# A one-core kernel of attention and two MoE layers: softmax reciprocals one group later, warm-up matmuls, a shared PSUM bank and one TensorE visit per attention group

## The chip, the cores and the metric

The kernel runs on one core of one Trainium2 chip. The metric is device time of one execution in microseconds (us), the median of a few runs. A core has TensorE (PE, the matmuls), VectorE (DVE), ScalarE (ACT), GpSimd (POOL) and SyncE (SP), which run side by side and meet at semaphores; DMA queues move data between DRAM and the on-chip SBUF. Matmul results stand in PSUM, 8 banks of 128 partitions by 2 KB.

## What is computed

Three stages follow each other, cut here to what matters:

```python
def _attn_ref(q_l, k_l, v_l, q_g, k_g, v_g):        # batch 4, 8 heads, 512 local + 32 global, D 64
    out_g = np.matmul(sm(scale * q_g @ k_all.T), v_all)
    s_ll = np.where(np.abs(pos[:, None] - pos[None, :]) <= 32, s_ll, -1e9)
    out_l = np.matmul(sm(np.concatenate([s_lg, s_ll], axis=-1)), np.concatenate([v_g, v_l], axis=2))
    return np.concatenate([out_g, out_l], axis=2)
def _moe_ref(x, w1, w2, w3, w_out):                  # 2304 tokens, 512 -> 768 -> 512
    return np.maximum(np.maximum(x @ w1, x @ w2), x @ w3) @ w_out
def _moe2_ref(x, w_in, w_out):                       # 512 -> 2048 -> 512
    h = x @ w_in
    return (np.maximum(h, 0.0) + np.log1p(np.exp(-np.abs(h)))) @ w_out
```

`sm` is a softmax that divides by the sum plus 1e-9. The weights are float64 in DRAM (two 32-bit words each).

## The kernel before

**Attention.** The work is cut into 32 groups (4 batches, 2 halves of the sequence, 4 pairs of heads), numbered k = 0 to 31. A group goes through steps that stand in different turns of one generator, `att_stream`: `s1` (PE scores ps, DVE adds the mask and takes the minimum, L155, four per group), `s1e` (ACT exponentials, L162), `s1f` (DVE reciprocals rs of the sums, L168 and L169, and POOL's two multiplications by them, L171 and L172), `s2` (PE transposes pw, L218, and pg, L219), `s2e` (ACT and DVE copy these to pgt and pwt), `s3` (PE output po, L245 and L249), `s3h` (ACT: high part xh of the output, or xo to DRAM) and `s3l` (DVE: low part xl, L270). Every second group also serves the global queries: `s1g` (PE psg), `gsoft` (its softmax, tile gsc), `g2` (PE transposes pb, L279, and pa, L283) and `g3` (PE output pog, L297).

**First MoE.** A product of float32 precision is made of three matmuls of high and low parts (L504 to L506 and L550 to L552). There are 8 units u of 256 or 288 token columns. `up` makes one of 18 products pu of a unit (6 slices f, 3 weights i), 12 matmuls each; `rest` takes the maximum over i (ACT copies the first, DVE L518 the others); `split_h` makes hh and hl of the maximum; `down` makes two output slices pd with 36 matmuls each, which ACT copies to o (L555).

**Decoder.** `dec_stream` turns 24 float64 weight tiles into two float32 parts. For each tile ACT takes a magnitude (L448), DVE makes four steps (L462, L465, L469, L473; the middle two in the PSUM tile pt), and ACT and POOL write the two parts of w (L442, L443).

**Order.** All engines' streams are issued in the order of the Python code. First, until the inputs of units 0 and 1 are there (groups 0 to 10, the *opening* below), the driver walks `att_stream` and, between its steps, hands out decode steps (`part`) and some `up`s of unit 0 (`slot`). Groups 0 to KS-1 run in a fused form with two stops per group; the others in an order written out as letters in `ORD`, each letter a step of its own. Then comes the *run*: the remaining `up`s of units 0 and 1 (36 in all) with 2.3 decode steps behind each. Then units 0 to 7 go through `up` and `down`, and `more` lets attention steps in between by a rate (RA per `up`, RD per `down`), until attention ends. The second MoE decodes its weights the same way.

**PSUM.** Pool pm has 5 banks for everything that comes from `ptile` and for pu, pd, pt, pw, pg, pa, pb and psg; pool pp holds ps (two banks) and one bank with the tag "o" for po and pog in turn.

Of the kernel before, what the change touches and what calls it, by code (L numbers as in the profile page):

```python
# [7 lines left out]
F32 = mybir.dt.float32  # L8
# [12 lines left out]
def body(ctx, tc, kq, vw, vb, qg, w1, w2, w3, w_out, w2_in, w2_out, out):  # L21
# [4 lines left out]
    WM = 0  # L26
    KL = 10
    KW = 9
    KS = 8
    ORD = 'AHaBbFDIEG'  # L30
    HHA = 2
    HLP = 2
# [5 lines left out]
    pm = mo_ctx.enter_context(tc.tile_pool(name="pm", bufs=5, space=PSUM))  # L38
# [7 lines left out]

    ident = const.tile([128, 128], F32, name="ident")
# [163 lines left out]
    def s2(k):  # L211
# [4 lines left out]
        pg = ptile([128, 128], "pg")  # L216
# [20 lines left out]
    def s3(k):  # L237
# [3 lines left out]
        po = pp.tile([128, 4, 64], F32, tag="o", name="po", bufs=1)  # L241
# [30 lines left out]
    def g2(b, s):  # L272
# [4 lines left out]
        pb = ptile([128, 128], "pb")  # L277
# [10 lines left out]
    def g3(b, s):  # L288
# [3 lines left out]
        po = pp.tile([128, 2, 32], F32, tag="o", name="pog", bufs=1)  # L292
# [14 lines left out]
    def att_stream():  # L307
# [16 lines left out]
        for k in range(n + 3):  # L324
# [3 lines left out]
            if k < KS:  # L328
# [11 lines left out]
                if q3 is not None:  # L340
                    s3h(q3)
                yield 2 if k > 1 else 4
                next(soft, None)
# [3 lines left out]
                if q2 is not None:  # L347
                    s2e(q2)
                s1f(k)
# [12 lines left out]
                yield 3  # L362
            else:
                for c in ORD:
                    if c in "AaBb":
                        if k < n:
                            (s1 if c in "AB" else s1e)(k, "AaBb".index(c) // 2)
                            if c in "ab":
                                yield 0
                        if c in "AB":  # L370
                            next(soft, None)
                    elif c == "H":
                        if late:
                            g3(*late.pop())
                            ng += 1
                            yield 0
                    elif c == "D":
                        while p3 < p2 and p3 <= k - 2:
                            s3(p3)
                            s3h(p3)  # L380
                            s3l(p3)
                            p3 += 1
                            yield 0
                    elif c == "F":
                        if k < n:
                            s1f(k)
                            yield 0
                        next(soft, None)
                    elif c == "G":
                        if k < n and k % 2 == 1:  # L390
                            s1g(k)
                            yield 0
                    elif c == "E":
                        while p2 <= min(k - 1, n - 1):
                            s2(p2)
                            s2e(p2)
                            p2 += 1
                            yield 0
                    elif c == "I" and 2 <= k < n + 2:
                        b, hf, pr = groups[k - 2]  # L400
                        if hf == 1 and pr % 2 == 1:
                            g2(b, pr // 2)
                            yield 0
                            late.append((b, pr // 2))
# [29 lines left out]
    def dec_stream(srcs, wpool, rpool, pre, raws, staged):  # L434
# [22 lines left out]
        for i in range(n):  # L457
# [6 lines left out]
            t2 = ptile([128, 512], "pt").bitcast(I32) if staged else t  # L464
# [61 lines left out]
    def split_h(u, f):  # L526
# [9 lines left out]
        (nc.gpsimd if HLP > u else nc.vector).tensor_tensor(hl[:, f, 0:n], m, hh[:, f, 0:n].bitcast(F32), op=ALU.subtract)  # L536
# [72 lines left out]
    with tc.manual_schedule():  # L609
# [7 lines left out]
        AD = 5  # L617
        D0 = 0.5
        D2 = 2.0
        D3 = 1.0  # L620
        NS = 1
        MG = 1
        F2 = 5
        F6 = 1.2
        F7 = 2.0
        CX = 0
        FD = 3
        RJ = 0.7
        RD = 2.0
        RA = 1.9  # L630
        au = [0]
        nx = [0.0]
        debt = [0.0]

        def step():
# [439 lines left out]
```

## Time and profile before

| | us |
|---|---|
| median of 3 runs (811.77 to 813.16) | 812.82 |
| the profiled execution | 813.12 |
| its span in the trace | 811.4 |
| PE busy in it | 778.8 |
| DVE, ACT, POOL busy | 524.2, 423.7, 173.6 |

The profiled execution is 0.3 us above the median, and its trace spans 811.4 us of it. The stages by the clock of the trace: the opening until 66.5, the run of `up`s of units 0 and 1 until 119.8, `down` of unit 0 and the split of unit 1 until 155.5, the rest of attention beside units 1 to 4 until 318.3, then the end of the first MoE and the second one. A busy time of PE counts a matmul as long as its modelled end; what it lacks to a stretch's length is idle time of PE.

### The profile page before, as it was taken

What the parts mean: (1) busy time and instruction counts of PE and PEld (TensorE: products, weight loads), DVE (VectorE), ACT (ScalarE), POOL (GpSimd) and SP (SyncE); (2) the same over time, 40 slices, a digit from 0 to 9 for tenths busy, and PEclk for the clock granted to TensorE, in tenths of its full rate; (3) what the DMA queues carried; (4) which work ended last, traced back from release to release, by engine and by line L of the source; (5) the groups of instructions that cost most, each with busy time, mean ns of one, the idle gap of its engine ahead of it and who ended that gap; (6) DMA issues with size and microseconds to landing.
All of it is one profiled execution on the core that took longest, in us unless ns stands there. A gap on an engine that the chain in (4) does not pass through costs nothing.

```text
span 811.4 us, 17312 instructions
## 1 busy us (share of the span) xinstructions
PE 778.8 (96%) x6600; PEld 730.4 (90%) x6600; DVE 524.2 (65%) x1350; ACT 423.7 (52%) x1032; POOL 173.6 (21%) x183
## 2 busy tenths in 40 slices
PE   5689988999999999999998999999999999999998
PEld 3578987988989998999998889988999999999998
DVE  5867962455454453377746455655437989999996
ACT  5744534433433441324322688888878744444443
POOL 4434533211211120022223033433312200000000
PEclk9999999999999999999999999999999999999999
DMA  9827314433433411526020445544625734444421
GB/s 339 311 87 256 148 53 123 141 123 101 147 108 112 153 48 48 205 107 214 15 65 15 165 151 170 179 158 155 210 88 179 247 95 130 130 131 130 130 80 65
DMA packets 72403, 111.89 MB, mean 138 GB/s; under 512 B 9984, under 2 KB 51840, under 8 KB 72320
## 3 DMA queue, kind: packets, MB, share of 16 engines
q1 hardware_dynamic: 72320, 110.78, 40.8%
q8 instruction: 52, 0.85, 0.4%
q14 instruction: 31, 0.25, 0.1%
HBM read 80.67 MB, written 30.08 MB: 136 GB/s over the span
## 4 chain that ended last, share of the span: by engine, by line
PE 86%; DVE 6%; ACT 3%; DMA 2%; issue 1%; POOL 0%; SPq 0%; DVEq 0%; ACTq 0%; POOLq 0%
PE pu L504 8%; PE ph L976 8%; PE ph L978 8%; PE ph L977 8%; PE pu L505 7%; PE pu L506 7%; PE mb L863 7%; PE mb L864 7%; PE mb L862 7%; PE pd L550 3%; PE pd L551 3%; PE pd L552 3%; PE ps L149 2%; ACT s L162 2%; PE po L245 2%; DMA raw<-in_w_dram 2%
## 5 line engine op out<-in xcount | busy, mean ns | idle before, releaser
L504 PE MATMUL pu<-xh,w 128*128 128x288 f32 (+1 forms) x576 | 172.3, 299 | 5.3 <-DVE tmp L473 4.8
L505 PE MATMUL pu<-xl,w 128*128 128x288 f32 (+1 forms) x576 | 167.4, 291 | 0.0
L506 PE MATMUL pu<-xh,w 128*128 128x288 f32 (+1 forms) x576 | 166.7, 289 | 0.0
L863 PE MATMUL mb<-wo,oh 128*128 128x256 f32 x480 | 135.8, 283 | 0.0
L864 PE MATMUL mb<-wo,ol 128*128 128x256 f32 x480 | 135.7, 283 | 0.0
L862 PE MATMUL mb<-wo,oh 128*128 128x256 f32 x480 | 135.2, 282 | 0.0
L504 PEld LDWEIGHTS pu<-xh,w 128*128 128x128 f32 x576 | 109.6, 190 | 11.0 <-issue 5.4
L976 PE MATMUL ph<-o,w 128*128 128x384 f32 (+1 forms) x320 | 115.2, 360 | 0.5 <-ACT o L555 0.5
L978 PE MATMUL ph<-o,w 128*128 128x384 f32 (+1 forms) x320 | 115.0, 360 | 0.0
L977 PE MATMUL ph<-o,w 128*128 128x384 f32 (+1 forms) x320 | 115.0, 359 | 0.0
L505 PEld LDWEIGHTS pu<-xl,w 128*128 128x128 f32 x576 | 109.8, 191 | 0.0
L506 PEld LDWEIGHTS pu<-xh,w 128*128 128x128 f32 x576 | 109.6, 190 | 0.0
L984 DVE SCALAR_TENSOR_TENSOR g<-ph,a 128x384 f32<-128x384 f32 (+1 forms) x80 | 48.8, 610 | 88.5 <-ACT a L983 64.0
L855 ACT ACTIVATE oh<-sm 128x640 fp32r<-128x640 f32 (+1 forms) x72 | 49.8, 692 | 89.6 <-DVE sm L850 83.8
L862 PEld LDWEIGHTS mb<-wo,oh 128*128 128x128 f32 x480 | 91.7, 191 | 0.0
L864 PEld LDWEIGHTS mb<-wo,ol 128*128 128x128 f32 x480 | 91.3, 190 | 0.0
L863 PEld LDWEIGHTS mb<-wo,oh 128*128 128x128 f32 x480 | 91.2, 190 | 0.0
L162 ACT ACTIVATE s<-s,nm 128x160 f32<-128x160 f32 x128 | 53.4, 419 | 56.4 <-DVE nm L155 56.3
L443 POOL TENSOR_TENSOR w<-tmp,w 128x512 fp32r<-128x512 f32 x40 | 53.1, 1328 | 128.9 <-ACT w L442 82.5
L518 DVE TENSOR_TENSOR m<-m,pu 128x256 f32<-128x256 f32 (+1 forms) x96 | 41.7, 434 | 56.4 <-PE pu L506 50.6
L171 POOL TENSOR_TENSOR s<-s,rs 128x512 f32<-128x512 f32 x32 | 33.4, 1044 | 165.1 <-DVE rs L169 87.8
L976 PEld LDWEIGHTS ph<-o,w 128*128 128x128 f32 x320 | 60.2, 188 | 6.5 <-ACT o L555 0.7
(125 smaller groups left out, 1584.7 us busy)
## 6 DMA issues: line engine op xcount, KB each, us to landing
gl<-gd SPq DMA_DIRECT2D x32, 512.0 KB, 5.1
kq<-in_kq_dram SPq DMA_DIRECT2D x31, 448.0 KB, 4.4
raw<-in_w_out_dram SPq DMA_DIRECT2D x22, 512.0 KB, 4.1
raw<-in_w_dram SPq DMA_DIRECT2D x18, 512.0 KB, 7.6
gd<-g SPq DMA_DIRECT2D x48, 192.0 KB, 2.5
vt<-in_vw_dram SPq DMA_DIRECT2D x16, 512.0 KB, 5.5
raw<-in_w_in_dram SPq DMA_DIRECT2D x16, 512.0 KB, 7.5
gd<-g SPq DMA_DIRECT2D x32, 256.0 KB, 3.9
```

The lines of the kernel that those rows point to most:

```text
L162: nc.scalar.activation(s[:, u, :], s[:, u, :], AF.Exp, scale=-1.0, bias=g["nm"][:, u:u + 1], accum_out=g["sm"][:, u:u + 1])
L443: nc.gpsimd.tensor_tensor(w[:, 1, :], tf, w[:, 0, :].bitcast(F32), op=ALU.subtract)
L504: nc.tensor.matmul(p, lhsT=w[:, 0, k], rhs=xh[:, k, 0:n], start=(k == 0), stop=False)
L505: nc.tensor.matmul(p, lhsT=w[:, 0, k], rhs=xl[:, k, 0:n], start=False, stop=False)
L506: nc.tensor.matmul(p, lhsT=w[:, 1, k], rhs=xh[:, k, 0:n], start=False, stop=(k == 3))
L855: nc.scalar.activation(oh[:, a:b], src, AF.Copy)
L862: nc.tensor.matmul(p, lhsT=oh[:, a], rhs=w[:, 0], start=st, stop=False, skip_group_check=True)
L863: nc.tensor.matmul(p, lhsT=oh[:, a], rhs=w[:, 1], start=False, stop=False, skip_group_check=True)
L864: nc.tensor.matmul(p, lhsT=ol[:, a], rhs=w[:, 0], start=False, stop=sp, skip_group_check=True)
L976: nc.tensor.matmul(p, lhsT=w[:, 0, k], rhs=oh[:, 0:n], start=(k == 0), stop=False)
L977: nc.tensor.matmul(p, lhsT=w[:, 0, k], rhs=ol[:, 0:n], start=False, stop=False)
L978: nc.tensor.matmul(p, lhsT=w[:, 1, k], rhs=oh[:, 0:n], start=False, stop=(k == 3))
```

## The change

1. **Fused form for groups 0 to 10** (KS from 8 to 11), and in it `s1f` of group k-1 stands behind the exponentials of group k (it stood behind those of its own group); `s2e` of the group before moves ahead of the stop at which decode steps are handed out.
2. **One visit per later group.** `ORD` is gone. From group 11 on, `s1`, `s3`, `s2` and `s1g` are issued in one step; the exponentials, `s1f`, `g3` and `g2` are the following steps. RD and RA, the rates at which steps are let in, go from 2.0 and 1.9 to 1.4 and 1.35, AD from 5 to 3.
3. **Warm-up matmuls.** 18 matmuls on `ones` at the start (WM), 12 behind the scores of group 0 and 6 behind those of group 1 (WB); no one reads their results.
4. **PSUM.** Pool pm has 4 banks, a new pool pt has one for the decoder's middle steps, and one bank `acc` is shared by po (columns 0 to 255), pg (256 to 383), pb (384 to 511) and pog (0 to 63).
5. **Decode steps of the opening.** No decode step in group 0, one in group 1, three per group to group 8, five in groups 9 and 10, with two `up`s behind each of these (NSL). Both kernels hand out 32 in the opening.
6. **hl of unit 0 and 1.** On POOL only for unit 0, f below 3; the nine others move to DVE (before, all twelve were on POOL).

```diff
-    KS = 8
-    ORD = 'AHaBbFDIEG'
+    KS = 11
...
-    pm = mo_ctx.enter_context(tc.tile_pool(name="pm", bufs=5, space=PSUM))
+    pm = mo_ctx.enter_context(tc.tile_pool(name="pm", bufs=4, space=PSUM))
+    pt = mo_ctx.enter_context(tc.tile_pool(name="pt", bufs=1, space=PSUM))
...
+    acc = pp.tile([128, 512], F32, tag="o", name="acc", bufs=1)
...
-        pg = ptile([128, 128], "pg")
+        pg = acc[:, 256:384]
...
-        po = pp.tile([128, 4, 64], F32, tag="o", name="po", bufs=1)
+        po = acc[:, 0:256].rearrange("p (u n) -> p u n", n=64)
...
-        pb = ptile([128, 128], "pb")
+        pb = acc[:, 384:512]
...
-        po = pp.tile([128, 2, 32], F32, tag="o", name="pog", bufs=1)
+        po = acc[:, 0:64].rearrange("p (a n) -> p a n", n=32)
...
+                if k:
+                    s1f(k - 1)
+                next(soft, None)
+                if q2 is not None:
+                    s2e(q2)
                 yield 2 if k > 1 else 4
-                next(soft, None)
                 if q3 is not None:
                     s3l(q3)
                     p3 += 1
-                if q2 is not None:
-                    s2e(q2)
-                s1f(k)
...
-                for c in ORD:
...
+                if k == KS:
+                    s1f(k - 1)
+                if k < n:
+                    s1(k, 0)
+                    s1(k, 1)
+                while p3 < p2 and p3 <= k - 2:
+                    s3(p3)
+                    s3h(p3)
+                    s3l(p3)
+                    p3 += 1
+                while p2 <= min(k - (2 if k == KS else 1), n - 1):
+                    s2(p2)
+                    s2e(p2)
+                    p2 += 1
+                if k < n and k % 2 == 1:
+                    s1g(k)
+                next(soft, None)
+                yield 0
+                for i in range(2):
+                    if k < n:
+                        s1e(k, i)
+                        yield 0
+                    next(soft, None)
+                if k < n:
+                    s1f(k)
+                    yield 0
...
-            t2 = ptile([128, 512], "pt").bitcast(I32) if staged else t
+            t2 = pt.tile([128, 512], F32, tag="t", name="t2").bitcast(I32) if staged else t
...
-        (nc.gpsimd if HLP > u else nc.vector).tensor_tensor(hl[:, f, 0:n], m, hh[:, f, 0:n].bitcast(F32), op=ALU.subtract)
+        (nc.gpsimd if u == 0 and f < HLP else nc.vector).tensor_tensor(hl[:, f, 0:n], m, hh[:, f, 0:n].bitcast(F32), op=ALU.subtract)
...
-                part(D2)
+                part(D2 if cnt < 8 else D2L)
...
-                part(D3 if cnt > 1 else 3.0)
-                for _ in range(NS):
+                part(D3 if cnt < 8 else D3L)
+                for _ in range(NS if cnt < 8 else NSL):
...
-                if cnt > 8 and au[0] and ready(0):
-                    flush()
-                    slot(0)
-            cnt += 1
+                cnt += 1
+            elif cnt == 0:
+                warm(WB)
```

The first place is DVE's stream from the start of the program. Before, the scores of groups 0 and 1 (L155), each followed by its reciprocals, then the decode steps of the first tile:

```order
L155 ISA nm 128x1
L168 TENSOR_SCALAR rs<-sm 128x4
L169 RECIPROCAL rs<-rs 128x4
L462 TENSOR_SCALAR tmp<-tmp 128x512
L155 ISA s,nm<-ps,mask 128x160
...
L168 TENSOR_SCALAR rs<-sm 128x4
L169 RECIPROCAL rs<-rs 128x4
L465 TENSOR_SCALAR pt<-tmp 128x512
L469 SCALAR_TENSOR_TENSOR pt<-raw,pt 128x512
L473 SCALAR_TENSOR_TENSOR tmp<-raw,pt 128x512
```

After, the scores of groups 0 and 1 stand together (the lines move by a few numbers; t_294 is the decoder's tile in its own bank):

```order
L156 ISA s,nm<-ps,mask 128x160
L156 ISA nm 128x1
...
L169 TENSOR_SCALAR rs<-sm 128x4
L170 RECIPROCAL rs<-rs 128x4
L156 ISA s,nm<-ps,mask 128x160
...
L169 TENSOR_SCALAR rs<-sm 128x4
L170 RECIPROCAL rs<-rs 128x4
L460 TENSOR_SCALAR tmp<-tmp 128x512
L463 TENSOR_SCALAR t_294<-tmp 128x512
```

The reciprocals now stand behind a whole group of scores, and the first decode step behind three groups.

The second place is PE between `up`s and `down`s of the first units. Before, a group's work comes in separate pieces between products pu:

```order
L245 MATMUL po<-pgt,vb 64x128 x4
L249 MATMUL po<-pwt,vt 64x64 x8
L504 MATMUL pu<-xh,w 128x256
...
L218 MATMUL pw<-ident,s 128x128 x4
L219 MATMUL pg<-ident,sg 128x128
L184 MATMUL psg<-kq,qg 64x256 x2
L504 MATMUL pu<-xh,w 128x256
...
L149 MATMUL ps<-kq 64x160 x8
```

After, the same pieces of a group stand in a row:

```order
L150 MATMUL ps<-kq 64x160 x8
L246 MATMUL acc<-pgt,vb 64x128 x4
L250 MATMUL acc<-pwt,vt 64x64 x8
L219 MATMUL pw<-ident,s 128x128 x4
L220 MATMUL acc<-ident,sg 128x128
L185 MATMUL psg<-kq,qg 64x256 x2
L502 MATMUL pu<-xh,w 128x256
```

Interruptions of the products by attention fall in number, and the transposes pw of a group now stand right behind the outputs po of the group before.

The third place is ACT behind `down` of unit 0. Before, the split of unit 1 (hh) came ahead of the copies of the attention's output:

```order
L162 ACTIVATE s,sm<-s,nm 128x160 x4
L533 ACTIVATE hh<-m 128x288 x6
L262 ACTIVATE xo<-po 128x256
L230 ACTIVATE pgt<-pg 128x128
L193 ACTIVATE gsc<-psg 128x288
L555 ACTIVATE o<-pd 128x288 x2
```

After:

```order
L553 ACTIVATE o<-pd 128x256 x2
L163 ACTIVATE s,sm<-s,nm 128x160 x2
L263 ACTIVATE xo<-acc 128x256 x2
L231 ACTIVATE pgt<-acc 128x128
L194 ACTIVATE gsc<-psg 128x288
L531 ACTIVATE hh<-m 128x288 x6
```

There the copies xo, pgt and gsc stand ahead of hh, which unit 1's `down` waits for.

## Rows read from the trace of the kernel before

**Rows 1.** Busy time by stretch: us, engines (count), PEclk, DMA share, GB/s

```profile
5.20:21.90 16.70, 11.04 (x124) 7.62 (x126) 11.88 (x52) 11.47 (x43) 5.90 (x8) 1.00 1.01 393
21.90:43.70 21.80, 15.07 (x209) 11.76 (x203) 17.45 (x66) 14.62 (x53) 11.88 (x14) 0.92 0.79 281
43.70:66.50 22.80, 20.52 (x297) 18.01 (x296) 15.45 (x56) 12.99 (x45) 6.25 (x7) 1.00 0.24 80
66.50:119.80 53.30, 48.50 (x363) 47.49 (x361) 45.31 (x86) 24.58 (x50) 27.43 (x24) 0.97 0.44 165
119.80:155.50 35.70, 32.90 (x353) 28.91 (x352) 12.22 (x54) 16.82 (x62) 10.32 (x14) 0.95 0.36 112
155.50:318.30 162.80, 161.43 (x1877) 145.99 (x1873) 79.96 (x299) 64.43 (x231) 24.82 (x34) 1.00 0.34 109
```

**Rows 2.** DVE in the run: start, us, line, operation [idle before <-releaser]

```profile
80.72 0.42 DVE L462 TENSOR_SCALAR tmp<-tmp 128x512 f32<-128x512 f32 x1
83.24 0.42 DVE L462 TENSOR_SCALAR tmp<-tmp 128x512 f32<-128x512 f32 x1
...
110.41 0.43 DVE L462 TENSOR_SCALAR tmp<-tmp 128x512 f32<-128x512 f32 x1 [1.80 <-ACT tmp L448]
```

**Rows 3.** PE at the end of the run

```profile
113.31 0.40 PE L504 MATMUL pu<-xh,w 128*128 128x288 f32 x1 [2.18 <-DVE tmp L473]
```

**Rows 4.** DVE in the opening: the scores of group 4, and one reciprocal's first half

```profile
21.96 0.31 DVE L155 CUSTOM_DVE_ANT_0 s<-ps,mask 128x160 f32<-128x160 f32 x1
...
29.08 0.92 DVE L168 TENSOR_SCALAR rs<-sm 128x4 f32<-128x4 f32 x1
```

**Rows 5.** DVE, groups of 21.9 to 66.5: shapes, count | busy us, mean ns | idle before

```profile
L168 DVE TENSOR_SCALAR rs<-sm 128x4 f32<-128x4 f32 x7 | 1.9, 276 | 1.6 <-ACT s L162 1.6
```

**Rows 6.** PE in the opening

```profile
38.55 0.66 PE L283 MATMUL pa<-ident,gsc 128*128 128x128 f32 x4 [1.80 <-DVE tmp L473]
...
40.10 0.41 PE L505 MATMUL pu<-xl,w 128*128 128x256 f32 x1
...
57.30 0.66 PE L245 MATMUL po<-pgt,vb 128*64 128x128 f32 x8 [1.77 <-DVE xl L270]
```

**Rows 7.** PE around one `down` of unit 2's stretch

```profile
200.13 0.39 PE L504 MATMUL pu<-xh,w 128*128 128x256 f32 x1
...
201.76 0.66 PE L245 MATMUL po<-pgt,vb 128*64 128x128 f32 x8
...
202.81 0.39 PE L550 MATMUL pd<-hh,w 128*128 128x256 f32 x1
203.03 0.28 PE L551 MATMUL pd<-hl,w 128*128 128x256 f32 x1
...
207.08 0.28 PE L552 MATMUL pd<-hh,w 128*128 128x256 f32 x1
```

**Rows 8.** POOL, groups of 0 to 160

```profile
L443 POOL TENSOR_TENSOR w<-tmp,w 128x512 fp32r<-128x512 f32 x24 | 30.9, 1289 | 35.3 <-ACT w L442 30.7 <-issue 4.6
L171 POOL TENSOR_TENSOR s<-s,rs 128x512 f32<-128x512 f32 x16 | 16.7, 1041 | 46.0 <-DVE rs L169 23.1 <-DVE gsm L206 9.7 <-ACT w L442 5.9
```

**Rows 9.** DVE, groups of 119.8 to 318.3

```profile
L518 DVE TENSOR_TENSOR m<-m,pu 128x256 f32<-128x256 f32 x21 | 8.8, 419 | 19.3 <-PE pu L506 16.3 <-ACT gsc L204 2.4 <-DMA kq<-in_kq_dram 0.6
...
L536 DVE TENSOR_TENSOR hl<-m,hh 128x256 fp32r<-128x256 f32 x10 | 4.3, 433 | 0.3
```

**Rows 10.** All engines at the split of unit 1

```profile
137.39 2.09 ACT L533 ACTIVATE hh<-m 128x288 fp32r<-128x288 f32 x6
...
137.87 0.40 PE L550 MATMUL pd<-hh,w 128*128 128x288 f32 x1 [0.62 <-ACT hh L533]
...
139.39 0.36 ACT L262 ACTIVATE xo<-po 128x256 f32<-128x256 f32 x1
139.43 4.57 POOL L536 TENSOR_TENSOR hl<-m,hh 128x288 fp32r<-128x288 f32 x6
...
140.27 0.40 PE L551 MATMUL pd<-hl,w 128*128 128x288 f32 x1 [2.00 <-POOL hl L536]
```

More of the change, by code (lines that the diff above doesn't have):

```diff
@@ L24, in body @@
     scale = 1.0 / float(D) ** 0.5
-    WM = 0
+    WM = 18
     KL = 10
     KW = 9
-    KS = 8
-    ORD = 'AHaBbFDIEG'
+    KS = 11
     HHA = 2
-    HLP = 2
+    HLP = 3
     XLP = 0
@@ L361, in att_stream @@
                         late.append((b, pr // 2))
-                yield 3
+                yield 3 if k else 4
             else:
-                for c in ORD:
[L365 to L404, printed above, removed]
@@ new lines, in att_stream @@
+                next(soft, None)
[8 more added lines that the diff above has]
+                    yield 0
+                for c in late:
+                    g3(*c)
+                    ng += 1
+                    yield 0
+                late = []
+                if k < n + 2:
+                    b, hf, pr = groups[k - 2]
+                    if hf == 1 and pr % 2 == 1:
+                        g2(b, pr // 2)
+                        late.append((b, pr // 2))
+                        yield 0
@@ L616, in body @@
         FJ = 2.3
-        AD = 5
-        D0 = 0.5
+        AD = 3
         D2 = 2.0
@@ L621, in body @@
         NS = 1
+        D2L = 3.0
+        D3L = 2.0
+        NSL = 2
+        WB = 6
         MG = 1
@@ L628, in body @@
         RJ = 0.7
-        RD = 2.0
-        RA = 1.9
+        RD = 1.4
+        RA = 1.35
         au = [0]
@@ L673, in body @@
                 au[0] += 1
-                continue
-            if v == 2:
+            elif v == 2:
                 flush()
-                part(D2)
-            elif v == 4:
-                continue
+                part(D2 if cnt < 8 else D2L)
             elif v == 3:
-                part(D3 if cnt > 1 else 3.0)
-                for _ in range(NS):
+                part(D3 if cnt < 8 else D3L)
+                for _ in range(NS if cnt < 8 else NSL):
                     if au[0] and ready(0):
                         slot(0)
-            else:
-                part(D0)
-                if cnt > 8 and au[0] and ready(0):
-                    flush()
-                    slot(0)
-            cnt += 1
+                cnt += 1
+            elif cnt == 0:
+                warm(WB)
         flush()
```

## The prediction

> **What bounds the kernel now.** I read the busy times by stretch first, then the idle time of PE inside the stretches, then the rows of the engine that ends each pause. PE is busy 778.8 of 811.4 us, so what can be won at once is the idle time, the slowed matmuls, and whatever a switch between kinds of matmul costs. The stretches [rows 1] say where. In 5.2 to 21.9 PE has work for 11.0 of 16.7 us, the DMA share is 1.01 and DVE is busy 11.9: the inputs of the first groups pace it. In 21.9 to 66.5 PE idles 9.0 us and DVE is busy 32.9 of 44.6, so idle 11.7. In the run, 66.5 to 119.8, DVE is busy 45.3 of 53.3, and most of its other time is two pauses near the end: one decoded tile takes 83.24 - 80.72 = 2.52 [rows 2], and 16 of them fill 40.3. DVE's decoding paces the run; a late tile costs PE 2.18 there [rows 3], because DVE itself had waited 1.80 for the magnitude of a tile whose raw words came late [rows 2]. Behind the run PE idles 2.8 in the split of unit 1, and from 155.5 to 318.3 only 1.4 in all [rows 1]. From 318.3 on the change leaves the order as it was, and I take those 493.1 us as they are; the pool of four PSUM banks is short only where more than four products stand open, which the lag of two does not make.
>
> The granted clock falls three times. It is 0.92 in 21.9 to 43.7, 0.97 in the run and 0.95 in 119.8 to 155.5 [rows 1]; a matmul of this kind that takes 0.28 at full clock [rows 7] takes 0.41 there [rows 6], so PE stood at the lower of its two levels (1.2 instead of 2.4 GHz). Each time a pause of 1.8 to 2.2 us lay a few us ahead [rows 3, 6, 10]. The price of one such fall is (1 - 0.92) x 21.8 = 1.7 us.
>
> The sum is made against the profiled execution, 813.1; the median of the runs is 0.3 lower.
>
> **Part 1, the opening and the run.** *What happens until group 4.* By the scores of group 4, which start at 21.96 [rows 4], DVE has done ten decode steps in the kernel before; in the new order it has five. That is 5 x 0.63 (a quarter of 2.52) = 3.15 less in front of it, and one reciprocal pair (0.35) less. The gain lies between 0 (the inputs set the pace: DMA share 1.01 [rows 1]) and 3.5. I take 1.3, nearer the lower end for that DMA row: group 4 at 20.7.
>
> The warm-up matmuls lie in time in which PE waits for these inputs, and I cost them at nothing; their cover is 5.7 us of idle PE in that stretch. If they bought full clock for the first groups' scores, these still wait for inputs: nothing either way, and at worst group 4 comes 0.8 later, which lies inside the bounds.
>
> *From group 4 to the run.* DVE was busy 32.9 there. The new order has 23 decode steps until the last input of unit 1 where there were 21 (+1.3), one copy pwt (-0.7) and one maximum (-0.4) less, and the reciprocal that took 0.92 instead of 0.17 [rows 4] is taken as normal (-0.7): 32.4. Of its idle 11.7, the 1.6 before reciprocals [rows 5] goes, since rs now stands a group behind its exponentials; the rest I leave in size. New waits arise in the shared bank: pog of groups 8 and 10 and pb of 9 have to wait until DVE has read the low part xl out of the bank, and xl stands behind the decode steps handed out at that stop. The nearest row is po waiting 1.77 for xl [rows 6], in the one bank that po and pog shared already. Waits of DVE of the same kind are in the 11.7, so I keep 10.1. The run's DVE part starts at 20.7 + 32.4 + 10.1 = 63.2.
>
> *The run.* Then 17 tiles remain (seven are done) at 2.52: 42.8. The maxima and the three hl that move to DVE there are 23; what one adds is at most (45.3 - 40.3)/19 = 0.26, so 6.0. The late raw words stay (two buffers as before): 1.8. DVE is done at 113.8; PE has 32 products left; the 30 of the run before kept it busy 48.5 [rows 1], 1.7 of it by the clock, so 1.56 each, 49.9 for 32, from 63 until 112.9, and DVE still sets the end. With its last product behind it the run ends near 114.2, against 119.8: -5.6. Pushed out of the opening into later stretches are one group's po (1.05) and pw (0.63): +1.7. And the three waits in the shared bank may each lower the clock as the pauses of the same size did: one at least for certain, all three 5.1, against one such fall that was there (1.7). I take +1.9. **Part 1: -2.0**, between -5 (group 4 at its best, no further fall) and +2.5 (group 4 no earlier, three falls).
>
> This page bears on the shared bank: the Trainium skill, "PSUM — Partial Sum Buffer", section "PSUM bank collisions raise a hardware error", says that TensorE, ScalarE and VectorE may not touch the same bank and quadrant at once, so that accesses are to be kept apart by bank. Here ACT's copy of pg and DVE's xl, which have banks of their own before, would have to take turns; the trace of before shows no such pair, and by the rule Part 1 would lie nearer to its upper end.
>
> **Part 2, fewer visits.** A visit of attention between products costs beyond its matmuls. On PE [rows 7] the product at 200.13 reaches the next po at 201.76: 1.63 for 12 matmuls spaced (207.08 - 203.03)/34 = 0.119, which is 1.43; 0.20 more. The 36 of `down` give 207.08 - 202.81 = 4.27 for 35 steps of 0.119, 0.11 more. The order has 50 visits before and 32 now: 18 x 0.17 (between the two, the row with a product being the commoner) = **-3.1**, from -2.0 (0.11) to -3.6 (0.20).
>
> **Part 3, a wait for POOL.** A group's reciprocals stand in the step just ahead of the visit that transposes its pw; between rs and pw lies POOL's multiplication, 1.04 [rows 8]. Where a maximum and a split stand ahead of rs on DVE, the chain from the last product is m 0.42, hh about 0.4, hl 0.43 [rows 9], rs 0.35, POOL 1.04 and 0.1 to 0.2 of signalling: 2.8. PE covers it with the scores (0.70) and po (1.05) in the same visit, so it would wait about 1.0. The order has that case once (group 20, ahead of unit 2's `down`); three visits (groups 13, 28, 29) come one product after their rs and I put 0.35 on each. The sum is 2.1. In return the pauses at the end of attention, part of the 1.4 idle of 155.5 to 318.3 [rows 1], mostly go: -0.9. **Part 3: +1.2**, from -0.9 (POOL early everywhere) to +3.1.
>
> **Part 4, unit 1's split.** Its `down` waited 0.62 for hh and 2.00 for hl on POOL [rows 10]; POOL took 0.76 for each of six hl, DVE takes 0.43 [rows 9], and hl on POOL queued behind the multiplications. The change puts it on DVE. But ACT's six hh now stand behind xo twice, pgt and gsc, about 0.35 each (xo takes 0.36, hh 2.09/6 [rows 10]): 1.4. So the pause falls from 2.6 to 1.4 and with it, I assume at 7 in 10, the fall of the clock (1.8 = 0.05 x 35.7): -1.2 - 1.3 = **-2.5**, from -0.5 to -3.6.
>
> **Sum.** -2.0 - 3.1 + 1.2 - 2.5 = -6.4: 813.1 - 6.4 = 806.7 for a profiled run, **806.4** as a median. The four half-widths (3.8, 0.8, 2.0, 1.6) give 4.6 together if they fall independently, so the forecast's own range is 802 to 810.8.
>
> **Rivals.** *B, the opening gives nothing back.* Group 4 is no earlier and the shared bank's waits add to DVE's idle, so Part 1 is +1.7, just the work pushed out. The DMA row speaks for it, the fuller DVE order against. 806.4 + 3.7 = 810.1. *C, the opening gains more.* DVE's idle halves (10.1 to 5.1), as its queue always holds something ready: 801.4. For it speaks that the pauses before were ends of chains ps, s, rs that now lie a group apart; against, the shared bank. *D, POOL slows the hl that move to DVE.* A reciprocal took 0.92 beside POOL instead of 0.17 [rows 4]; POOL writes a w for 1.29 of every 2.52 [rows 8]. If each of the run's three hl loses the like, 1.1 at most, that is 3.4 on the engine that paces: 809.8. By the Trainium skill, "SBUF — State Buffer", section "Who interferes with whom", a VectorE instruction with two SBUF inputs gets in the way of GpSimd's SBUF traffic, and hl is one; the rs row (one input) already shows a loss. *E, the wait for POOL comes at nine visits,* wherever rs and the next visit are neighbours or a product apart: 9 x 1.0 in place of 2.1, +6.9: 813.3, no change. *F, slower, by the shared bank alone.* Each of three turns (pog, pb, pog) costs PE and DVE 1.77, the row of po, and a fall of the clock of 1.7: 10.4 on top of -5.6 + 1.7. Part 1 is then +6.5 and the time 814.9. It decides from +6.0. The waits are real in the order; against it, DVE has decode steps to do while it waits, and only the one fall is known.
>
> That the change does not do what it says (the warm-up leaves PE as slow until 19 us as before) costs nothing that is not inside Part 1.
>
> **How the numbers follow.** Forecast 0.50, B 0.15, C 0.13, D 0.08, E 0.06, F 0.08. The range runs from C, 801.0, to 812.5: above it lie E and F, some 0.14, and a little of C lies below. About 0.2%, 1.6 us, is what a measurement of this kernel can tell from no change: faster means under 811.2, slower over 814.4. Faster has the forecast (0.48 of 0.50), C and most of B and D: 0.80. The same: E and the tails, 0.11. Slower: F and a tail, 0.09.
>
> **What would show it.** Scores of group 4 near 20.7; the run of products from about 63 to 114, DVE without pauses in it but the one of the raw words; between products PE visits that all begin with ps; at the split of unit 1 a pause of about 1.4 and no DVE wait. The prediction is wrong if DVE's idle between 21 and 63 grows beyond 13, if PEclk falls more than twice before 114, or if pw waits for POOL at many visits.

## The result, and the profile after

The changed kernel takes 823.23 us (median of four runs, 821.42 to 824.43) against 812.3 (four, 811.6 to 813.16): the ratio is 1.0132, with a 95% interval of 1.0109 to 1.0156. It is slower by 10.9 us, where a gain of 6.4 was forecast. Its profiled execution took 824.43, of which the trace spans 822.7. The busy times of the engines (the page's first part):

```profile
PE 790.0 (96%) x6636; PEld 739.9 (90%) x6636; DVE 524.8 (64%) x1357; ACT 422.7 (51%) x1034; POOL 164.9 (20%) x174
```

PE's busy time grew by 11.2 us, while its matmuls are the same but for 36. The warm-up matmuls account for about 8; the rest are matmuls at the lower clock and waits that lie under a matmul's modelled end. The stretches that answer to [rows 1], cut at the changed kernel's own borders (start of the run at 68.4, its end at 123.5, end of unit 1's `down` at 160.9, end of attention at 338.8), in the columns of [rows 1]:

```profile
5.20:21.90 16.70, 15.18 (x141) 11.02 (x140) 7.71 (x43) 9.45 (x39) 4.19 (x6) 1.00 1.02 387
21.90:43.70 21.80, 14.72 (x238) 12.03 (x239) 19.06 (x76) 15.71 (x58) 9.78 (x11) 1.00 0.73 264
43.70:68.40 24.70, 17.56 (x221) 14.83 (x220) 14.06 (x47) 12.67 (x44) 8.74 (x10) 0.87 0.70 256
68.40:123.50 55.10, 52.16 (x390) 50.65 (x388) 47.61 (x91) 23.89 (x47) 22.19 (x18) 0.96 0.24 85
123.50:160.90 37.40, 33.95 (x370) 30.00 (x370) 14.95 (x64) 19.00 (x67) 8.93 (x11) 0.95 0.35 109
160.90:338.80 177.90, 173.48 (x1974) 157.12 (x1973) 81.68 (x308) 65.89 (x240) 24.78 (x36) 0.99 0.33 105
```

The third row is the worst: 7.1 of 24.7 us idle on PE, and DVE busy only 14.1. PE's rows of that time (start, us, operation, idle before and its releaser), beside [rows 6]:

```profile
39.71 0.31 PE L280 MATMUL acc<-ident,gsc 128*96 128x128 f32 x1 [2.85 <-DVE xl L271]
...
46.32 1.84 PE L298 MATMUL acc<-gt,vt 128*64 128x32 f32 x40 [2.00 <-DVE xl L271]
...
57.03 0.31 PE L280 MATMUL acc<-ident,gsc 128*96 128x128 f32 x1 [2.71 <-DVE xl L271]
...
65.52 2.92 PE L298 MATMUL acc<-gt,vt 128*64 128x32 f32 x40 [2.43 <-DVE xl L271]
```

L280 is pb and L298 is pog. Each of the four waits for DVE to read xl out of the shared bank: 10.0 us together. In the kernel before the four longest pauses of PE from 35 to 70 are 1.80, 0.52, 1.77 and 0.51, 4.6 together (the first and the third stand in [rows 6]), and none of them stands ahead of a pb or a pog. The pog at 65.52 takes 2.92 instead of 1.84: the clock has fallen.

DVE's rows from then on (the scores of group 4, which answer to [rows 4], and the waits around the run) show the other end of these pauses:

```profile
22.71 0.32 DVE L156 CUSTOM_DVE_ANT_0 s<-ps,mask 128x160 f32<-128x160 f32 x1
...
68.74 0.23 DVE L110 TENSOR_TENSOR xl<-acc,xh 128x64 fp32r<-128x64 f32 x1 [3.28 <-ACT xh L109]
71.33 0.42 DVE L516 TENSOR_TENSOR m<-m,pu 128x256 f32<-128x256 f32 x1 [1.31 <-PE pu L504]
73.25 0.42 DVE L516 TENSOR_TENSOR m<-m,pu 128x256 f32<-128x256 f32 x1 [1.49 <-PE pu L504]
...
103.74 0.42 DVE L534 TENSOR_TENSOR hl<-m,hh 128x256 fp32r<-128x256 f32 x1 [0.48 <-ACT hh L531]
...
118.65 0.43 DVE L460 TENSOR_SCALAR tmp<-tmp 128x512 f32<-128x512 f32 x1 [1.68 <-ACT tmp L446]
```

While PE waits for DVE, DVE soon runs dry itself, 3.28 at the last turn. In the later groups PE's rows show three single pauses of over 1 us that were not there before:

```profile
127.12 0.33 PE L220 MATMUL acc<-ident,sg 128*128 128x128 f32 x1 [1.23 <-ACT xo L263]
...
209.91 0.66 PE L219 MATMUL pw<-ident,s 128*128 128x128 f32 x4 [1.05 <-POOL s L172]
...
290.19 0.67 PE L246 MATMUL acc<-pgt,vb 128*64 128x128 f32 x8 [2.10 <-DMA vb<-in_vb_dram]
```

Between run end and the end of unit 4's `down`, by when all or nearly all attention is done in both, the changed kernel takes 219.7 us (123.5 to 343.2) and the one before 212.9 (119.9 to 332.8). So the loss has two parts: 3.7 until the end of the run, where a gain of 3.7 was forecast (5.6 less 1.9 for the clock), and 6.8 behind it, where a gain of 2.7 was forecast (the 1.7 of work pushed out of the opening, and Parts 2 to 4). Two falls of the clock lie behind the run, from 147.4 and from 290.7, for 3.4 us each; the kernel before has one there, from 142.1.

### The profile page after: what moved, and what is told of

Read it like the earlier page. It is cut to its first block, busy times and chain, and to the rows that moved or that the text cites. A ratio compares the mean times of both kernels' runs of the same rounds, so it can differ in the third digit from the quotient of the medians.

```text
span 822.7 us, 17383 instructions
## 1 busy us (share of the span) xinstructions
PE 790.0 (96%) x6636; PEld 739.9 (90%) x6636; DVE 524.8 (64%) x1357; ACT 422.7 (51%) x1034; POOL 164.9 (20%) x174
## 4 chain that ended last, share of the span: by engine, by line
PE 83%; DVE 10%; ACT 2%; DMA 2%; issue 2%; POOL 1%; SPq 0%; POOLq 0%; DVEq 0%; ACTq 0%
PE ph L971 7%; PE ph L972 7%; PE ph L973 7%; PE pu L502 7%; PE mb L859 7%; PE mb L857 7%; PE mb L858 7%; PE pu L504 7%; PE pu L503 7%; PE pd L549 3%; PE pd L548 3%; PE pd L550 3%; PE ps L150 2%; PE acc L298 2%; PE pw L219 2%
## 5 line engine op out<-in xcount | busy, mean ns | idle before, releaser
L502 PE MATMUL pu<-xh,w 128*128 128x256 f32 (+1 forms) x576 | 170.8, 297 | 1.9 <-DVE m L516 1.2
L504 PE MATMUL pu<-xh,w 128*128 128x256 f32 (+1 forms) x576 | 167.2, 290 | 1.0 <-POOL w L441 1.0
L503 PE MATMUL pu<-xl,w 128*128 128x256 f32 (+1 forms) x576 | 167.8, 291 | 0.0
L973 PEld LDWEIGHTS ph<-o,w 128*128 128x128 f32 x320 | 60.2, 188 | 5.7
L972 PEld LDWEIGHTS ph<-o,w 128*128 128x128 f32 x320 | 60.2, 188 | 5.7
```

What stands on the lines that cost most here:

```text
L502: nc.tensor.matmul(p, lhsT=w[:, 0, k], rhs=xh[:, k, 0:n], start=(k == 0), stop=False)
L503: nc.tensor.matmul(p, lhsT=w[:, 0, k], rhs=xl[:, k, 0:n], start=False, stop=False)
L504: nc.tensor.matmul(p, lhsT=w[:, 1, k], rhs=xh[:, k, 0:n], start=False, stop=(k == 3))
L972: nc.tensor.matmul(p, lhsT=w[:, 0, k], rhs=ol[:, 0:n], start=False, stop=False)
L973: nc.tensor.matmul(p, lhsT=w[:, 1, k], rhs=oh[:, 0:n], start=False, stop=(k == 3))
```

## The experiments

Ratios are to the kernel before, run on the same chip beside it; times of different chips are not compared. A run from the changed kernel is read against its 1.0132, one from the kernel before against 1. A trace is of one execution, and executions of one kernel differ in their falls of the clock; a fall of 3.4 us at half the clock costs up to 1.7, an estimate that is used below. Where two traces are compared, their falls are named.

**One part undone or done alone.** `a1_banks` gives the changed kernel the banks of before:

```diff
-    pm = ... bufs=4 ...
-    pt = ... bufs=1 ...
+    pm = ... bufs=5 ...
-    acc = pp.tile([128, 512], F32, tag="o", name="acc", bufs=1)
-        pg = acc[:, 256:384]
+        pg = ptile([128, 128], "pg")
```

(po, pb, pog and the decoder's tile likewise.) 

> The changed kernel with the PSUM banks of the kernel before: pm has five banks and serves the decoder's middle steps, pg and pb too; po and pog alone take turns in one bank. Theory S (the shared bank is the loss: in the changed kernel PE's four pauses for xl ahead of pb and pog in the opening last 10.0 us where those of before last 4.6, one more fall of the clock costs 1.7, and ahead of pg, po and pw in the later groups PE loses some 6 to ACT's copies): 810 to 817. Theory W (the warm-up matmuls and the fewer decode steps ahead of group 4 are the loss): 820 or more.

Measured: 1.0092 (1.0061 to 1.0123), 818.2. A third of the loss goes, by the middle values. Theory S is right in kind and wrong in size: 818.2 lies above its 810 to 817. Two things stay. pog still shares with po, as before, and in the fused form xl stands behind the decode steps, so PE's row still reads

```profile
45.45 2.07 PE L296 MATMUL pog<-gt,vt 128*64 128x32 f32 x40 [2.00 <-DVE xl L269]
...
62.12 1.84 PE L296 MATMUL pog<-gt,vt 128*64 128x32 f32 x40 [2.43 <-DVE xl L269]
```

and a pause that has nothing to do with banks grew to 3.47 (vb, below).

`a2_nowarm` sets WM and WB to 0. 

> The changed kernel without its 36 warm-up matmuls. Theory W (their 8.25 us of PE time delay the first scores: group 0 at 5.2 instead of 3.7 us, group 1 at 9.2 instead of 6.4): 817 to 820. Theory S (they lie in time in which PE waits for inputs, since group 4's scores come at 20.0 in the changed kernel and at 20.4 before): 822 to 824.5.

Measured: 1.0115 (1.0089 to 1.0142), 819.9, so 0.0017 less; the intervals overlap, and only `c3_own_vb_nowarm` below settles it. In its trace the scores of group 4 come to DVE at 20.50 instead of 22.71.

`b2_banks` puts the new banks into the kernel before. 

> The kernel before with the banks of the changed one alone: pm four banks, the decoder's middle steps in a bank of their own, po, pg, pb and pog in one shared bank. Theory S: slower by 4 or more, 816 to 823, since pg stands behind ACT's copy of po and po behind pg's copy in the old order as well. Rival (the shared bank hurts only in the order of one visit, where po and pg stand side by side): 811 to 814.

Measured: 1.0105 (1.0072 to 1.0137), 819.2: the banks alone cost about 8 us in the old order too. PE waits there 3.34 ahead of pb at 40.44 and 3.23 ahead of pg at 144.73, and PEclk is down to 0.82 from 43.7 to 70.

`b1_visit` gives the kernel before the one-visit order from group 11 on, RD 1.4, RA 1.35 and AD 3. 

> The kernel before with the one-visit order alone, from group 11 on, with its rates (1.4 and 1.35) and its three steps ahead of unit 0; banks, opening and hl as before. Theory V (fewer visits give back about 3 us, waits for POOL take 1 to 2 of it): 808 to 811.5. Rival (the order itself makes waits that eat it, 2 us and more): 813 to 817.

Measured: 0.9960 (0.9944 to 0.9976), 807.7 beside 811.0. Theory V holds: this part alone is faster by 3.3, and from the run's end to unit 4's `down` its trace takes 209.0 us instead of 212.9, with one fall of the clock there in both. At unit 1's split its rows are

```profile
137.83 0.40 PE L586 MATMUL pd<-hh,w 128*128 128x288 f32 x1 [0.87 <-ACT hh L569]
138.76 0.40 PE L587 MATMUL pd<-hl,w 128*128 128x288 f32 x1 [0.53 <-POOL hl L572]
```

against 0.62 and 2.00 [rows 10]: most of the pause ahead of hl goes with the order, with hl still on POOL.

`b3_open` gives the kernel before the opening alone (fused form to group 10, late reciprocals, its decode steps, products and warm-up matmuls). 

> The kernel before with the opening of the changed one alone: fused form for groups 0 to 10, reciprocals a group later, its decode steps, products and warm-up matmuls; banks, later order, rates and hl as before. Theory O (the opening gives nothing back: its run of products ends where that of before ends, and 1.7 us of a group's po and pw are pushed behind it): ratio 1.002 to 1.004, 813 to 814.5. The forecast's own step (Part 1 without the shared bank, -3.9): 0.995 or less.

Measured: 1.0084 (1.0061 to 1.0108); both theories miss it. The run ends at 121.8, and then the old order, handed a group that is one step further behind, waits 2.13 ahead of a pg and 5.15 ahead of a po (139.21 and 146.42 in its trace). The opening and the later order can't be judged apart this way.

`b4_hl` is `b1_visit` with the changed kernel's nine hl on DVE; `b5_hl1` puts only the six of unit 1 there:

```diff
-        (nc.gpsimd if HLP > u else nc.vector).tensor_tensor(hl[:, f, 0:n], ...
+        (nc.gpsimd if u == 0 else nc.vector).tensor_tensor(hl[:, f, 0:n], ...
```

> The kernel before with the one-visit order (as in the run before, 807.7, ratio 0.9960) and in addition nine of twelve hl of units 0 and 1 on DVE. Forecast's Part 4 (a pause of 1.2 and a fall of the clock go): ratio 0.993 to 0.995. Rival (with the one-visit order the pauses ahead of unit 1's down are only 0.9 and 0.5 already, and hh on ACT is what it waits for): 0.9955 to 0.997.

> The kernel before with the one-visit order, and hl on DVE for unit 1 alone (six of twelve; the three of unit 0 in the run stay on POOL). If putting hl on DVE pays behind the run and costs in it (in the run before this one the run ended 1.5 later and unit 1's down 3.2 sooner after it): ratio 0.9925 to 0.994, some 807. Rival (DVE's part of the run has no room to give back, the loss there came from elsewhere): 0.995 to 0.997.

Measured: 0.9953 (0.9935 to 0.9972) and 0.9903 (0.9871 to 0.9935). The first can't be told from `b1_visit`. In its trace unit 1's `down` ends 30.8 us behind the run's end instead of 34.0, some 1.7 of it the fall from 141.2 that `b1_visit` has and `b4_hl` has not. But the run itself ends at 121.2, where that of `b1_visit` ends at 119.6 and that of `b5_hl1` at 117.9: in `b4_hl` DVE's three hl (0.42 or 0.43 each) wait 0.48 each for their hh on ACT, 2.7 in all. (`b1_visit` and `b5_hl1` are the same up to there; the former has a fall from 113.9 that the latter has not, and `b4_hl` has one from 80.5.) Without these three the ratio is lower by 0.005, on another chip and with a wider interval.

`b6_rs` is `b1_visit` with the reciprocals of groups 0 to 7 one group later. 

> The kernel before with the one-visit order, and in groups 0 to 7 the reciprocals one group later, nothing else of the opening changed. The forecast took 1.6 us of DVE's idle time ahead of the reciprocals as gained: ratio 0.993 to 0.9945. Rival (DVE only waits elsewhere for the same inputs, and pw of a group comes later): 0.9955 to 0.998.

Measured: 0.9907 (0.9878 to 0.9936), 805.0. The late reciprocals gain, more than forecast; the scores of group 4 come to DVE at 21.38 in its trace instead of 22.38, and the run ends at 116.1. That is 3.5 earlier than in `b1_visit`, and 1.8 earlier than in `b5_hl1`, whose opening is the same as that of `b1_visit` and whose run has no fall either. The 1.6 of idle ahead of reciprocals [rows 5], which the forecast took as gained, does not go: from 21.9 to 60 both `b1_visit` and `b6_rs` show 1.4. A gain lies ahead of group 4, where PE waits 0.6 ahead of group 3's scores instead of 1.9 (its pause at 13.5 in the two traces).

**Which tenant of the bank.** `a7_pg` takes pg alone out of the shared bank of the changed kernel, `a8_pbpog` takes out pb and pog:

```diff
-        pb = acc[:, 384:512]
+        pb = ptile([128, 128], "pb")
-        po = acc[:, 0:64].rearrange("p (a n) -> p a n", n=32)
+        po = ptile([128, 64], "pog").rearrange("p (a n) -> p a n", n=32)
```

> The changed kernel with pg alone taken out of the shared bank into pool pm; po, pb and pog still share. Theory G (half of the shared bank's price is pg behind ACT's copy of po: 0.15 to 0.2 us in each of some 20 later visits, and single waits of 1.2 and 0.3): ratio to before 1.0085 to 1.0105 where the changed kernel has 1.0132. Theory P (the price is the four pauses of the opening and the clock behind them): 1.0115 to 1.0135.

> The changed kernel with pb and pog taken out of the shared bank into pool pm; po and pg still share, as pg and po do in every group. Theory P: the four pauses of 2.0 to 2.9 ahead of pb and pog shrink to 0.5 or less, and with them the falls of the clock behind them: ratio 1.006 to 1.010. Theory G: 1.0115 or more.

Measured: 1.0077 (1.0051 to 1.0103) and 0.9953 (0.9930 to 0.9976). Two lines turn the slower kernel into one that is faster than before. By the middle values Theory P's place is worth 0.018 of the ratio and Theory G's 0.0055; both are more than either expected. The stretches of `a8_pbpog`:

```profile
21.90:43.70 21.80, 17.05 (x280) 13.82 (x280) 21.02 (x80) 17.73 (x67) 11.17 (x13) 1.00 0.75 268
43.70:63.00 19.30, 18.55 (x223) 16.25 (x222) 15.70 (x51) 12.35 (x40) 9.77 (x10) 1.00 0.90 337
63.00:115.00 52.00, 47.74 (x389) 45.61 (x387) 45.63 (x87) 23.51 (x47) 21.44 (x18) 1.00 0.25 86
```

PEclk is 1.00 in all three, DVE is busy 21.0 of 21.8, no pause ahead of pb or pog is over 0.5, and the run ends at 111.2 instead of 123.5: 12.3 us, of which the pauses are 9 or so. The rest fits the two falls of the opening, though no run has the pauses without the falls.

**The other half.** `a3_vb` issues the second vb load of each batch a group earlier (`k % 8 in (0, 1)`), and `a6_three` joins that with the banks of before and no warm-up matmuls.

> The changed kernel with the second of each batch's two vb loads issued one group earlier. Theory L (unit 4 loses 3.8 us there: po of group 26 waits 2.10 for the DMA of its vb, which SP issues behind a later group's xo than before, and the clock falls for 3.4 us behind that pause): 1.0046 times less than the changed kernel's 1.0132, so ratio 1.0086, about 819. Rival (the pause is covered by something else that is late as well): 1.012 to 1.0135.

> The changed kernel with three things undone or mended at once: banks of before, no warm-up matmuls, vb one group earlier. If the three losses add up (3.5 for banks, 1.8 for warm-up matmuls, and with the old banks 3.5 + 3.4 for the vb wait and its clock): ratio 0.998, some 809. If they cover each other: 1.004 or more.

Measured: 1.0129 (1.0099 to 1.0159) and 0.9977 (0.9955 to 0.9999). The first looks like a miss of Theory L: the pause of 2.10 for vb is gone from its trace, and the time is the same. Its PEclk is 0.81 and 0.82 in the two stretches from 21.9 to 68.4, where the changed kernel's profile had 1.00 and 0.87, so what it gave back later it had lost in falls of the clock ahead of 77: its run ends 3.8 later than that of the changed kernel, and from there to the end of unit 4's `down` it takes 4.2 less, without the falls from 147.4 and 290.7. A wait of 0.64 is left there, for vt. With the old banks, where the vb pause was 3.47 and the clock fell for 6.8 us behind it, the forecast ratio of 0.998 came out.

To settle it without the opening's falls, three runs start from the changed kernel with pg, pb and pog all in pm: `c1_own` alone, `c2_own_vb` with the earlier load, `c3_own_vb_nowarm` without warm-up matmuls as well.

> The changed kernel with pg, pb and pog in pool pm, so that po has its bank to itself; all else as changed. Theory G (pg waits 0.15 to 0.2 for ACT's copy of po in some 20 later visits, and 1.2 once): 4 less than with pb and pog alone taken out (809.2, ratio 0.9953), so ratio 0.990 to 0.992. Rival (those waits only move, since pm's four banks are then shorter): 0.994 to 0.997.

> The same with the second vb load of each batch one group earlier. Theory L (2.1 of waiting and 1.7 of clock at 274 to 281): 3 to 4 less than the run before it, ratio 0.985 to 0.988. Rival (it showed nothing alone and shows nothing here): within 0.001 of it.

> The same without the warm-up matmuls as well. If the warm-up delays the opening by its first scores (0.6 to 1.5 us): 0.001 to 0.002 less than the run before it. If it keeps the clock up in the opening (the run with pb and pog taken out shows no fall before 277): the same or 0.002 more.

Measured, on one chip: 0.9946 (0.9931 to 0.9961), 0.9899 (0.9884 to 0.9914), 0.9863 (0.9849 to 0.9878). The step to `c2_own_vb` is 0.0047, 3.6 us, as much as Theory L said, but the traces give the load only part of it:

```profile
276.34 0.66 PE L246 MATMUL acc<-pgt,vb 128*64 128x128 f32 x8 [2.94 <-DMA vb<-in_vb_dram]
```

```profile
274.08 0.69 PE L250 MATMUL acc<-pwt,vt 128*64 128x64 f32 x16 [1.51 <-DMA vt<-in_vw_dram]
```

The wait of 2.94 for vb in `c1_own` becomes one of 1.51 for vt in `c2_own_vb`, so of the 2.7 that `c2_own_vb` takes less from the run's end to unit 4's `down`, some 1.3 is the load. The other 1.4 lies far ahead of it, behind a fall of the clock from 135.2 that only `c1_own` has. Whether the long wait brings falls of its own is not shown by this pair. The step to `c3_own_vb_nowarm` is 0.0036, 3.0 us, more than forecast by either theory: its run ends 2.8 earlier, and the wait for vt is gone as well.

On Theory G the time of `c1_own` speaks for the rival, 0.994 to 0.997. But its trace has a fall of the clock in the opening (from 22.6) that `a8_pbpog` does not have, and its run ends 1.7 later. From the run's end to unit 4's `down`, with one fall there in each, `c1_own` takes 213.8 us and `a8_pbpog` 217.4: 3.5 less, though its wait for vb is 0.9 longer. `a7_pg` takes 212.4 there with no fall, the changed kernel 219.7 with two. So pg's waits cost about 4 behind the run, with the falls put at 1.7 each, and the later end of the run hides nearly half of that in the time of `c1_own`. The rows show where pg waits. The four transposes pw and the pg behind them, in the changed kernel and in `c1_own`:

```profile
162.60 0.66 PE L219 MATMUL pw<-ident,s 128*128 128x128 f32 x4
163.24 0.30 PE L220 MATMUL acc<-ident,sg 128*128 128x128 f32 x1
```

```profile
160.32 0.66 PE L219 MATMUL pw<-ident,s 128*128 128x128 f32 x4
160.81 0.27 PE L220 MATMUL pg<-ident,sg 128*128 128x128 f32 x1
```

pg starts 0.64 behind pw in the one and 0.49 in the other. Over the 23 later visits the difference is 4.3 us between `a8_pbpog` and `c1_own`; 0.8 of it is the first visit, where it shows as idle time (1.23 against 0.44), and the other 3.5 hardly shows as idle time, since the wait lies under the modelled end of pw.

The stretches of `c3_own_vb_nowarm`:

```profile
21.90:43.70 21.80, 17.32 (x266) 14.06 (x267) 19.63 (x72) 17.92 (x66) 11.64 (x14) 1.00 0.75 261
...
56.00:110.00 54.00, 50.90 (x391) 49.17 (x388) 48.61 (x93) 25.23 (x51) 24.41 (x20) 1.00 0.36 132
110.00:145.00 35.00, 32.20 (x370) 28.69 (x373) 15.14 (x64) 18.98 (x68) 9.08 (x11) 1.00 0.38 116
145.00:315.40 170.40, 168.92 (x1973) 155.15 (x1969) 81.45 (x308) 65.94 (x240) 24.71 (x36) 1.00 0.34 109
```

At 801.0 it is the best of all: 11.5 us faster than the kernel before and 2.7% faster than the changed one. `c4_rs_hl1` comes to it from the other side, the kernel before with the one-visit order, the late reciprocals and hl of unit 1 on DVE.

> The kernel before with the one-visit order, hl of unit 1 on DVE and the reciprocals of groups 0 to 7 a group later; banks, decode steps and products of the opening as before, no warm-up matmuls. Alone the last two stand at 0.9903 and 0.9907 on the one-visit order's 0.9960. If they add: 0.985 to 0.987, 800 to 801.5. If both only removed the same pause: 0.990.

Measured: 0.9877 (0.9861 to 0.9894), 802.4, between the two. By the middle values the two steps give 0.0083 together where they gave 0.0057 and 0.0053 alone: about three quarters of the sum, on different chips.

## Why the prediction was wrong

Of the 16.8 us between 806.4 and 823.2, 7.4 lie ahead of the run's end (forecast at 114.2 and 1.9 for the clock, measured at 123.5) and 9.5 behind it.

**The step that failed first is the 10.1 us of DVE idle in Part 1.** I saw that pb and pog would wait for xl, and counted three waits as lying inside the idle time that was already there. They are four, 10.0 us on PE, and DVE runs dry behind them. From the scores of group 4 to the end of the last pog (22.71 to 68.44) DVE is busy 32.3, as forecast (32.4), and idle 13.4. In `a8_pbpog` (22.71 to 57.22) it is idle 3.3. So pb and pog in the shared bank cost 10.1 us there (13.4 less 3.3), and were put at nothing beyond the old idle time, while the idle time that I carried over from the old order mostly goes with that order. The run then takes 55.1 where 51.0 was forecast (63.2 to 114.2), since DVE waits 1.31 and 1.49 for products made behind the fall of the clock at 65.4, and three times 0.48 for hh; in `a8_pbpog` it takes 54.0.

Rival F is this mechanism. It had the right place and the right price of one fall; its 1.77 for a turn was too little (2.0 to 2.9) and it had three of four, so it stood at 814.9 and 0.08. Its Part 1 would end the run at 124.6; it ended at 123.5. F deserved more: the order shows what stands ahead of xl at each turn, three instructions of 0.58 to 0.70, two or three of them decode steps, so about 2 us could be read off, where I took the one row of po. The falls were 10.2 us at the lower clock (3.4 and 6.8) until the run's end, against 6.8 before.

Had these waits been absent, Part 1 would have been too small a gain, not too large: `a8_pbpog` ends its run at 111.2, where 114.2 plus 1.9 for clock was forecast. Behind the run `c3_own_vb_nowarm`, without falls there, takes 209.8 until unit 4's `down`, 3.1 less than the kernel before with its one fall, where a gain of 2.7 was forecast.

**Two costs behind the run I did not have.** Ahead of pg, the shared bank makes PE wait for ACT's copy of po, 0.15 to 0.20 in most later visits and once 1.23. I spoke of the rule of the Trainium skill, "PSUM — Partial Sum Buffer", section "PSUM bank collisions raise a hardware error", that engines are to be kept apart by bank, but for ACT against DVE only, and priced it in the opening alone. Here it is PE that waits, 4.3 us in 23 visits (`a8_pbpog` against `c1_own`). And a load: vb for group 26 is issued in the row

```profile
283.96 0.42 SPq L89 DMA_DIRECT2D vb<-in_vb_dram  x1
```

by SP, behind the output copies of unit 3's `down`; `b1_visit` issues the same load at 269.83, ahead of the second half of them. The changed kernel stands one part of a group further back at that point, so the load fell behind the whole of the `down`. I counted the 1.7 of work that was pushed out of the opening, and did not follow what its being late does to SP's queue. The wait is 2.10, and behind it the clock falls from 290.7 for 3.4 us, an estimated 1.7; in `a7_pg` and `c1_own` the like wait brings no fall.

**Part 1's start** was wrong by 2 us: group 4's scores came at 22.71, later than the 21.96 of before and not at 20.7. The warm-up matmuls, costed at nothing, account for nearly all of it: with them group 0's scores start at 5.2 instead of 3.7, and without them group 4's come at 20.50 in `a2_nowarm`, at 21.26 in `a6_three`, and in `c3_own_vb_nowarm` near the forecast:

```profile
20.88 0.32 DVE L156 CUSTOM_DVE_ANT_0 s<-ps,mask 128x160 f32<-128x160 f32 x1
```

Leaving them out is worth 0.0036 there. I took idle PE time as their cover, but the idle time lies between the scores, and PE takes them in order.

**Part 2 and Part 3 held in their sum, and gave a little more.** Together they were to give 1.9; `b1_visit` gives 3.3 (2.0 to 4.5), part of it from unit 1's split. The one full wait for POOL came where the order puts it (209.91, 1.05 against "about 1.0"), and pw's waits for POOL sum to 2.1 in the changed kernel, the forecast's own sum. The 0.17 for a visit was not measured by itself.

**Part 4 was half right.** The pause ahead of hl goes from 2.00 to 0.53 by the new order, before any hl moves. In the changed kernel it is gone and 0.87 is left ahead of hh (forecast: 1.4), yet the clock fell there all the same, from 147.4; in `b5_hl1` it did not. hl on DVE for unit 1 gains, and for unit 0 it costs in the run, where I had put 0.26 for each and not its wait for hh.

Of the other rivals, D did not come: the run's three hl took 0.42 to 0.43, the 0.43 of [rows 9], since none of them met a POOL instruction; what happens where one does stands below. E did not come either, and C, the opening that gains more, came true in the opening as soon as pb and pog left the bank: DVE's idle time there is 3.3, less than the 5.1 of C.

None of the three signs that were to show the prediction wrong came: DVE was idle 10.4 from 21 to 63, PEclk fell twice before 114, and pw waited for POOL at three later visits. The first was tied to clock times, and the idle time came later than that; counted to the start of the run it is over 13.

What stays open: what decides whether a pause brings a fall of the clock, and so how much of the time of single runs the falls are.

## What to carry to other kernels

When tiles are made to share a PSUM bank, list for each its readers, and what stands ahead of each reader on its own engine; the wait is about the length of that list, and it repeats at each turn. Idle time of the old order is no allowance for it: here that idle time went with the old order. A part that is moved back also moves its loads in SP's order, so look at what they fall behind. And where a change has six parts, the parts that gain can hide in one that loses: here two lines in one of six parts made 1.8% of difference.

## What the hardware showed that I had not expected

A pause of some 2 us is followed by a fall of the granted clock, or not. The changed kernel's profile has four pauses of 2.0 to 2.9 in the opening and two falls (at 48.4 for 3.4 us, at 65.4 for 6.8); `a3_vb`, with nearly the same pauses (2.8, 1.6, 2.5, 2.4), has three falls behind them, of 3.4, 6.8 and 6.8 us, and one of 6.8 ahead of them, at 22.0. Shorter pauses are no safeguard: in the changed kernel 0.48, 0.76 and 0.87 within 5 us are followed by the fall at 147.4, and in `c3_own_vb_nowarm` the same three are not. There, with 1.5 as the longest pause from 16 to 430 us, the clock does not fall before 799. So a pause costs its length and, at times, an estimated 1.7 to 3.4 more (half of a fall's length), and kernels that differ only in such pauses are best compared by several runs.

The first 14 to 18 us run at half rate while PEclk reads 1.00: group 3's scores take 1.34 to 1.35 in the kernel before, in the changed one and in `c3_own_vb_nowarm`, and group 4's 0.77. With the warm-up matmuls PE left that state sooner in six of eight traces (group 3's scores at 15.6 take 0.77 to 0.98), and in each of these six the clock fell at 22.0 to 22.9, behind the pause of 1.7 to 1.8 that all eight have at 20.8; in the two others (the changed kernel, `a8_pbpog`) it did neither. In these six the early speed that the warm-up bought was lost a few us later.

POOL can slow DVE instructions that read and write SBUF alone, and left the maxima, which have an input in PSUM, as they were. In `b4_hl` one hl of a late unit stands in POOL's way:

```profile
337.10 0.31 DVE L571 CAST hh<-m 128x288 fp32r<-128x288 f32 x1
337.21 1.36 POOL L479 TENSOR_TENSOR w<-tmp,w 128x512 fp32r<-128x512 f32 x1 [29.99 <-ACT w L478]
337.44 1.44 DVE L572 TENSOR_TENSOR hl<-m,hh 128x288 fp32r<-128x288 f32 x1
338.81 0.41 DVE L498 TENSOR_SCALAR tmp<-tmp 128x512 f32<-128x512 f32 x1
```

It takes 1.44 where the other 23 of its shape, none of them beside POOL for more than half its time, take 0.45 to 0.54; the maxima m, whose second input is in PSUM, take 0.39 to 0.46 with or without POOL. The Trainium skill, "SBUF — State Buffer", section "Who interferes with whom", says that a DVE instruction with two SBUF inputs contends with a GpSimd instruction that reads SBUF; hl and m agree with it here. Moving work of this kind from POOL to DVE is safe only where POOL rests.
